# Rotating three key tiles on GpSimd and filling more TensorE waits with unread products in a fused attention and two-MLP kernel

## The chip, the core and the metric

One NeuronCore of a Trainium2 chip runs the whole program. The metric is the device time of one execution in microseconds (us), the median of several runs.

## What is computed

Attention with rotated queries and keys for 4 batches of 8 heads (576 tokens, 64 columns per head), then a two-layer MLP behind a layer norm (512 to 2048 to 512, with a residual), then a second, gated MLP that mixes tokens. All in fp32. The part that the change touches is the attention:

```python
def rotate(x):
    x1, x2 = (x[..., :half], x[..., half:])
    return np.concatenate([x1 * cos - x2 * sin, x1 * sin + x2 * cos], axis=-1)
q_rot, k_rot = (rotate(q), rotate(k))
scores = scale * np.matmul(q_rot, k_rot.transpose(0, 1, 3, 2))
scores = scores - np.max(scores, axis=-1, keepdims=True)
attn = np.exp(scores)
attn = attn / (np.sum(attn, axis=-1, keepdims=True) + 1e-09)
return np.matmul(attn, v)
```

## The kernel before

**Work.** A batch is a "group" g (0 to 3; batch 1 of the title is g = 0). Its 8 heads are 4 head pairs p; two heads lie on partitions 0 to 63 and 64 to 127. The queries of a pair are cut into hi = 0 (tokens 0 to 383, three units of 128) and hi = 1 (tokens 384 to 575, one unit of 128 and one of 64, which holds both heads as `qd`). A block is one pair and one half. In batch 1 the blocks run in the order hi = 0 for pairs 1 to 4 (blocks 0 to 3), then hi = 1 for pairs 1 to 4; in the other batches both halves of a pair follow each other. Only hi = 0 blocks load and rotate keys, so blocks 0 to 3 hold all the keys of batch 1.

**One unit.** TensorE (PE) makes the scores S of each head (L300, two products of 288 columns into the one PSUM tile of that head, S0 or S1). VectorE (DVE) takes the row maximum (L328). ScalarE (ACT) writes exp(S - max) into P with the row sums (L337), which frees the score tile. PE transposes P in blocks (L372) into the one PSUM tile T, ACT copies T to PT (L396, L403, L407), and when all of a block is there PE multiplies with the values (PV, L473). In the hi = 0 blocks of batch 1 (`ALONE`) the two heads of a unit run one after the other, the PV tile is one of the two PSUM tiles `m` of the MLP (`mps`), and the reciprocals of the row sums come by three PE transposes (inv, L491) and a multiplication on DVE (L496). In all other blocks they go to DRAM and back through DMAs on the GpSimd (POOL) queue (L436 to L447), and DVE multiplies at L484.

**Keys and queries.** `k_task` in `prep` loads both halves of a pair's keys as `kin` (L207, SP queue, two buffers), multiplies with cos and sin (L218, 1152 columns), adds the two halves into K (L220, 576 columns) and writes a second copy of the last 64 tokens (L226). The kin buffer is given back after that. `q_task` does the like for the queries (L252, L255, L263). All of it is on DVE.

**Around it.** 32 pieces of the MLP weights come in double precision and are turned into two fp32r parts (`convert`: ACT L58, L60, L733, DVE L62, L735, with loads `cd` and stores `wsc` on SP). When the four hi = 0 blocks of batch 1 are done, the layer norm of its first 288 tokens starts (`ln`: PE L604 with the ones matrix into the T tile, DVE L609, L618, ACT L629); the first MLP products follow (`up`, L754 to L756, then `down`, L784 to L786).

**What sets the order.** Everything is recorded by a planner (`Sched`) that runs while the kernel is built. Each task tells its engine, its earliest time and a cost in us; the planner always takes the step that can start first, and among those that could start within a fraction of it the one of lower rank. `UNIT`, `TURN`, `EVAC`, `VAL`, `NORM` and `REST` hold these ranks by batch: scores, transposes, copies of T, values, layer norm. The order so found is fixed on each engine; on the chip an instruction waits for its semaphores, and whatever is behind it on its engine waits too. Where the planner foresees that PE will wait, it calls `steady`, which records products of the `ones` matrix whose result nobody reads: 18 at the start, and later as many as the foreseen wait allows at 0.11 us each. They go into the `m` tiles. Before the change it does so only until the first values product has been recorded (`attn.pv`).

Of the kernel before, what the change touches and what calls it, by code (L numbers as in the profile page):

```python
# [10 lines left out]
ALU = mybir.AluOpType  # L11
# [11 lines left out]
FILL = 18  # L23
HOLD = 0.3
SWITCH = 0.3
ALONE = ((0, 0),)
UNIT = [2.25, 2.5, 2.25, 1.25]
EVEN = [9, 1, 1, -1]
RANK = dict(end=-1, convert=4.5, prep=3, load=3.5, loader=0.25)
NORM, REST = [0, 0.25, 1.5, 4], [2.75, 2.25, 3.5, 2.75]  # L30
TURN, EVAC, VAL = [2.25, 2.5, 2.5, 4.5], [1.25, 1.5, 0.25, 0.5], [2.75, 0.25, 1.75, 0.75]
FG = [4, 8, 8, 4]

AHEAD = 2
# [108 lines left out]
def latest(*xs):  # L143

    return None if any(x is None for x in xs) else max(xs)


class Attn:
# [42 lines left out]
    def prep(self, bi):  # L191

        nc, c, B = self.nc, self.c, self.blocks[bi]
        cs = self.k["cs"]
        parts = list(zip(KC, KC[1:])) if bi == 0 else [(0, 576)]
        s0, s1 = SPAN[B["hi"]]
        n = s1 - s0

        def k_task():
            e = yield "SP", self.kin.free, 0.7  # L200
            slot = self.kin.take()
            kin = self.p.tile([128, 2, 576], F32, tag="kin", name="kin")
            at = []
            for i, (a, z) in enumerate(parts):
                if i:
                    e = yield "SP", 0.0, 0.7
                nc.sync.dma_start(out=kin[:, :, a:z], in_=self.k["k"][B["b"], B["p"]][:, :, a:z])  # L207
                at.append(e + (3.5 if len(parts) > 1 else 7.5))
                if bi == 0:
                    e = yield "SP", 0.0, 0.6  # L210
                    q_load(*((0, 128), (128, 384))[i])
            for i, (a, z) in enumerate(parts):
                yield "DVE", lambda: latest(at[i], self.K.free() if i == 0 else 0.0), 0.0
                if i == 0:
                    B["kslot"] = self.K.take()
                    B["K"] = self.p.tile([128, 640], F32, tag="K", name="K", bufs=KB)
                yield "DVE", 0.0, 0.15 + 0.0021 * (z - a)
                nc.vector.tensor_tensor(kin[:, :, a:z], kin[:, :, a:z], cs[:, :, a:z], ALU.mult)  # L218
                e = yield "DVE", 0.0, 0.15 + 0.00105 * (z - a)
                nc.vector.tensor_tensor(B["K"][:, 64 + a:64 + z], kin[:, 0, a:z], kin[:, 1, a:z], ALU.add)  # L220
                if bi == 0:
                    if i == 0:
                        B["k0"] = e + 0.1
                        yield from q_turn((0, 128), at[0] + 0.6)
            e = yield "DVE", 0.0, 0.22
            nc.vector.tensor_tensor(B["K"][64:128, 0:64], kin[64:128, 0, 512:576], kin[64:128, 1, 512:576], ALU.add)  # L226
            B["k"] = e + 0.1
            self.kin.give(slot, e)
            if bi == 0:
                yield from q_turn((128, 384), at[1] + 0.6)  # L230

        def q_load(a=0, z=n):
            if a == 0:
                B["qslot"] = self.qin.take()
                B["Q"] = self.p.tile([128, 2, 384], F32, tag="qin", name="qin", bufs=QB)
            nc.sync.dma_start(out=B["Q"][:, :, a:z], in_=self.k["q"][B["b"], B["p"]][:, :, s0 + a:s0 + z])

        def q_turn(span, at):
            a, z = span
            t = B["Q"]  # L240
            yield "DVE", at, 0.15 + 0.0021 * (z - a)
            nc.vector.scalar_tensor_tensor(t[:, :, a:z], t[:, :, a:z], 0.125, cs[:, :, s0 + a:s0 + z], op0=ALU.mult, op1=ALU.mult)
            e = yield "DVE", 0.0, 0.15 + 0.00105 * (z - a)
            nc.vector.tensor_tensor(t[:, 0, a:z], t[:, 0, a:z], t[:, 1, a:z], ALU.add)
            B["q" if a else "q0"] = e + 0.1
# [20 lines left out]
        if B["newk"]:  # L266
            c.task(k_task(), 0.1 if bi == 0 else RANK["prep"] + 0.01 + 0.02 * bi)
# [16 lines left out]
    def unit(self, i, heads=None):  # L284
# [28 lines left out]
        if not after:  # L313
            c.task(self.unit(i, (1,)), UNIT[g])
        if after:
# [7 lines left out]
            if i + 1 < len(self.units):  # L323
                c.task(self.unit(i + 1), UNIT[self.units[i + 1]["g"]])
        nb, at = u["nb"], u["at"]
# [198 lines left out]
def fused_kernel(ctx, tc, q, k, v, cs, cst, w12, wi, wo, wsg, wsg4, gb, out):  # L524
    nc = tc.nc
    B = q.shape[0]
# [35 lines left out]
    mpsb = Bank(2)  # L562
    attn_ctx = ExitStack()
    attn = Attn(tc, attn_ctx, dict(q=q, k=k, v=v, cs=csb, ident=ident, x0=get_x0, x0_free=x0_free, mps=mps, mpsb=mpsb, dram=dram), groups, C)
# [8 lines left out]

    def steady(a, z):

        if attn.pv or z - a < 0.25:
            return
        n, r = (FILL, 128) if a < 1.0 else (int((z - a - 0.1) / 0.11), 64)
        for i in range(n):
            if i % 4 == 0:  # L580
                ps = mps.tile([128, 512], F32, tag="m", name="m")
            c = 128 * (i % 4)
            nc.tensor.matmul(ps[:, c:c + 128], ones[0:r], ones[0:r], start=True, stop=True)
# [104 lines left out]
    for g in range(NG):  # L688
        n = FG[g]
# [539 lines left out]
```

## Time and profile before

| | us |
|---|---|
| median of 3 runs (lowest, highest) | 916.14 (915.33, 917.90) |
| the profiled execution | 921.93 |
| its span, first to last instruction | 920.2 |

| engine | busy us (share of the span) | instructions |
|---|---|---|
| PE, matmul | 905.6 (98%) | 7206 |
| PE, weight load | 794.9 (86%) | 7206 |
| DVE | 586.0 (64%) | 1226 |
| ACT | 496.9 (54%) | 1132 |
| POOL | 107.4 (12%) | 212 |

The chain of waits that ended last is PE for 93% of the span. A busy PE is not the same as a PE at its peak: the ends of products are modelled, and short waits between them count as busy. A timeline row gives start, duration, engine, line, operation, tiles and shape, the count of records merged into it, and in brackets the idle time before it with what ended that. An fp32 product that is written once in the program shows as two records.

### The profile page before, as it was taken

The numbers are of one execution on the slowest core, as the hardware profiler recorded it, in microseconds if no ns is written. First come the engines' busy times: TensorE is split into PE (matmuls) and PEld (weight loads), VectorE is DVE, ScalarE is ACT, GpSimd is POOL, SyncE is SP. The second block draws the span as 40 slices with busy tenths as digits, with TensorE's granted clock in tenths as the row PEclk, the third lists the DMA queues.
The fourth block names the chain that finished last, engine by engine and source line by source line (L and its number), as shares of the span: only waits on it lengthen the run. The fifth ranks groups of instructions, "written<-read, shape, count | busy, mean of one in ns | idle before, by whom it ended". The sixth has DMA issues, their size and how long they took to land.

```text
span 920.2 us, 18252 instructions
## 1 busy us (share of the span) xinstructions
PE 905.6 (98%) x7206; PEld 794.9 (86%) x7206; DVE 586.0 (64%) x1226; ACT 496.9 (54%) x1132; POOL 107.4 (12%) x212
## 2 busy tenths in 40 slices
PE   9998999999999999999999999999999999999998
PEld 8556777777997887899778889999999999999998
DVE  6868776867686644358665316763435887776754
ACT  4989878768336655534455533464313746373520
POOL 0004321223001322300313220000000000000000
PEclk9989999999999999999999999999999999999999
DMA  8456536666472644257426333988651201203011
GB/s 319 164 181 226 197 111 218 214 231 240 186 223 74 199 146 139 80 187 236 136 77 213 101 105 122 325 287 273 211 178 40 65 2 50 66 1 104 1 52 53
DMA packets 64854, 138.81 MB, mean 151 GB/s; under 512 B 13056, under 2 KB 36224, under 8 KB 64768
## 3 DMA queue, kind: packets, MB, share of 16 engines
q1 hardware_dynamic: 57152, 132.96, 43.0%
q0 software_dynamic: 6784, 4.01, 1.8%
q8 instruction: 57, 0.93, 0.4%
q10 hardware_dynamic: 832, 0.66, 0.2%
q14 instruction: 29, 0.24, 0.1%
HBM read 110.43 MB, written 26.28 MB: 149 GB/s over the span
## 4 chain that ended last, share of the span: by engine, by line
PE 93%; ACT 4%; DMA 1%; DVE 1%; issue 0%; POOL 0%; POOLq 0%; DVEq 0%
PE S L300 10%; PE PV L473 8%; PE m L754 8%; PE m L784 8%; PE m L785 7%; PE m L786 7%; PE m L756 7%; PE m L755 7%; PE T L372 5%; PE p L1062 2%; PE p L1060 2%; PE p L1061 2%; PE p L1159 2%; PE p L1160 2%; PE p L1144 2%; PE p L1143 2%
## 5 line engine op out<-in xcount | busy, mean ns | idle before, releaser
L328 DVE TENSOR_REDUCE nb<-S 128x1 f32<-128x576 f32 x144 | 103.9, 751 | 79.8 <-PE S L300 79.0
L754 PE MATMUL m<-xh,w 128*128 128x288 f32 x480 | 147.9, 308 | 2.8 <-DVE h L764 2.8
L784 PE MATMUL m<-h,w 128*128 128x288 f32 x480 | 146.7, 306 | 0.0
L785 PE MATMUL m<-h,w 128*128 128x288 f32 x480 | 142.3, 297 | 0.0
L755 PE MATMUL m<-xl,w 128*128 128x288 f32 x480 | 141.8, 295 | 0.1
L756 PE MATMUL m<-xh,w 128*128 128x288 f32 x480 | 141.1, 294 | 0.0
L786 PE MATMUL m<-h,w 128*128 128x288 f32 x480 | 140.7, 293 | 0.0
L396 ACT COPY PT<-T 128x1024 f32<-128x1024 f32 (+5 forms) x120 | 75.2, 647 | 79.7 <-PE T L372 79.3
L764 DVE SCALAR_TENSOR_TENSOR h<-m,h 128x288 fp32r<-128x288 f32 x128 | 58.4, 456 | 86.4 <-ACT h L762 85.6
L337 ACT ACTIVATE P<-S,nb 128x576 f32<-128x576 f32 x144 | 106.7, 745 | 11.7 <-DVE nb L328 11.0
L762 ACT ACTIVATE h<-m 128x288 fp32r<-128x288 f32 x128 | 52.4, 410 | 92.5 <-PE m L756 91.3
L300 PE MATMUL S<-K,qin 64*128 64x288 f32 x512 | 96.3, 434 | 5.8 <-ACT P L337 5.6
L754 PEld LDWEIGHTS m<-xh,w 128*128 128x128 f32 x480 | 89.9, 187 | 9.4 <-DVE h L764 4.6
L436 POOL DMA_DIRECT2D inv<-st x112 | 57.3, 518 | 334.7 <-DVE st L432 334.4
L784 PEld LDWEIGHTS m<-h,w 128*128 128x128 f32 x480 | 90.4, 188 | 5.8 <-issue 2.1
L785 PEld LDWEIGHTS m<-h,w 128*128 128x128 f32 x480 | 90.8, 189 | 0.3
L755 PEld LDWEIGHTS m<-xl,w 128*128 128x128 f32 x480 | 90.2, 188 | 0.9 <-DVE xl L618 0.3
L786 PEld LDWEIGHTS m<-h,w 128*128 128x128 f32 x480 | 90.6, 189 | 0.0
L756 PEld LDWEIGHTS m<-xh,w 128*128 128x128 f32 x480 | 90.3, 188 | 0.0
L473 PE MATMUL PV<-PT,vin 128*64 128x384 f32 (+1 forms) x640 | 88.6, 419 | 0.0
L372 PEld LDWEIGHTS T<-ident,P 64*128 64x128 f32 x1312 | 58.7, 139 | 22.9 <-issue 8.8
L300 PEld LDWEIGHTS S<-K,qin 64*128 64x128 f32 x512 | 51.1, 188 | 25.2 <-ACT P L337 10.4
(154 smaller groups left out, 1849.6 us busy)
## 6 DMA issues: line engine op xcount, KB each, us to landing
w<-wsc SPq DMA_DIRECT2D x96, 512.0 KB, 4.0
cd<-in_w SPq DMA_DIRECT2D x32, 512.0 KB, 5.2
wsc<-w SPq DMA_DIRECT2D x24, 512.0 KB, 4.1
kin<-in_k SPq DMA_DIRECT2D x15, 576.0 KB, 6.4
vin<-in_v SPq DMA_DIRECT2D x20, 320.0 KB, 4.2
qin<-in_q SPq DMA_DIRECT2D x15, 384.0 KB, 6.3
x1d<-x SPq DMA_DIRECT2D x32, 144.0 KB, 2.8
x<-x1d SPq DMA_DIRECT2D x32, 144.0 KB, 2.8
```

The costliest lines, as they stand in the source:

```text
L300: nc.tensor.matmul(S[j][:, n, :], q, Kb["K"][r, a:a + HQ], start=True, stop=True)
L328: nc.vector.tensor_reduce(nb[:, j:j + 1], S[j], AX.XY, ALU.max, negate=True)
L337: nc.scalar.activation(P[:, 576 * j:576 * j + 576].rearrange("p (n k) -> p n k", n=2), S[j], AF.Exp, bias=nb[:, j:j + 1], scale=1.0, accum ...
L372: nc.tensor.transpose(ps[:, j, 64 * n:64 * n + 64], x["tile"][r, 128 * i:128 * i + 128], self.k["ident"][r, r])
L396: copy(t[:, i:i + n, q0:q0 + 128].rearrange("p c (j q) -> p j c q", j=2), ps[:, :, 64 * s:64 * s + 64 * n].rearrange("p j (c q) -> p j c q ...
L473: nc.tensor.matmul(ps[r, 0:n], V["vin"][:, ch, r], t[:, 4 if ch == 4 else 5 * j + ch, 0:n], start=ch == 0, stop=ch == 4)
L754: nc.tensor.matmul(ps, w[:, 0, ms], xh[:, kc, :], start=kc == 0, stop=False)
L755: nc.tensor.matmul(ps, w[:, 0, ms], xl[:, kc, :], start=False, stop=False)
L756: nc.tensor.matmul(ps, w[:, 1, ms], xh[:, kc, :], start=False, stop=kc == 3)
L784: nc.tensor.matmul(ps, w[:, 0, ms], t[:, 0, :], start=a == 0, stop=False)
L785: nc.tensor.matmul(ps, w[:, 1, ms], t[:, 0, :], start=False, stop=False)
L786: nc.tensor.matmul(ps, w[:, 0, ms], t[:, 1, :], start=False, stop=a == n - 1)
```

## The change

```diff
--- before.py
+++ after.py
@@ -24,11 +24,12 @@
 HOLD = 0.3
 SWITCH = 0.3
 ALONE = ((0, 0),)
-UNIT = [2.25, 2.5, 2.25, 1.25]
+GK = (1, 2, 3)
+UNIT = [2.25, 1.75, 2.25, 1.25]
 EVEN = [9, 1, 1, -1]
 RANK = dict(end=-1, convert=4.5, prep=3, load=3.5, loader=0.25)
 NORM, REST = [0, 0.25, 1.5, 4], [2.75, 2.25, 3.5, 2.75]
-TURN, EVAC, VAL = [2.25, 2.5, 2.5, 4.5], [1.25, 1.5, 0.25, 0.5], [2.75, 0.25, 1.75, 0.75]
+TURN, EVAC, VAL = [2.25, 2.5, 2.5, 4.5], [-1, 1.5, 0.25, 0.5], [2.75, 0.25, 1.75, 0.75]
 FG = [4, 8, 8, 4]
 
 AHEAD = 2
@@ -197,6 +198,7 @@
         n = s1 - s0
 
         def k_task():
+            eng, ve, f = ("POOL", nc.gpsimd, 2.0) if bi in GK else ("DVE", nc.vector, 1.0)
             e = yield "SP", self.kin.free, 0.7
             slot = self.kin.take()
             kin = self.p.tile([128, 2, 576], F32, tag="kin", name="kin")
@@ -210,20 +212,20 @@
                     e = yield "SP", 0.0, 0.6
                     q_load(*((0, 128), (128, 384))[i])
             for i, (a, z) in enumerate(parts):
-                yield "DVE", lambda: latest(at[i], self.K.free() if i == 0 else 0.0), 0.0
+                yield eng, lambda: latest(at[i], self.K.free() if i == 0 else 0.0), 0.0
                 if i == 0:
                     B["kslot"] = self.K.take()
                     B["K"] = self.p.tile([128, 640], F32, tag="K", name="K", bufs=KB)
-                yield "DVE", 0.0, 0.15 + 0.0021 * (z - a)
-                nc.vector.tensor_tensor(kin[:, :, a:z], kin[:, :, a:z], cs[:, :, a:z], ALU.mult)
-                e = yield "DVE", 0.0, 0.15 + 0.00105 * (z - a)
-                nc.vector.tensor_tensor(B["K"][:, 64 + a:64 + z], kin[:, 0, a:z], kin[:, 1, a:z], ALU.add)
+                yield eng, 0.0, f * (0.15 + 0.0021 * (z - a))
+                ve.tensor_tensor(kin[:, :, a:z], kin[:, :, a:z], cs[:, :, a:z], ALU.mult)
+                e = yield eng, 0.0, f * (0.15 + 0.00105 * (z - a))
+                ve.tensor_tensor(B["K"][:, 64 + a:64 + z], kin[:, 0, a:z], kin[:, 1, a:z], ALU.add)
                 if bi == 0:
                     if i == 0:
                         B["k0"] = e + 0.1
                         yield from q_turn((0, 128), at[0] + 0.6)
-            e = yield "DVE", 0.0, 0.22
-            nc.vector.tensor_tensor(B["K"][64:128, 0:64], kin[64:128, 0, 512:576], kin[64:128, 1, 512:576], ALU.add)
+            e = yield eng, 0.0, f * 0.22
+            ve.tensor_tensor(B["K"][64:128, 0:64], kin[64:128, 0, 512:576], kin[64:128, 1, 512:576], ALU.add)
             B["k"] = e + 0.1
             self.kin.give(slot, e)
             if bi == 0:
@@ -573,9 +575,9 @@
 
     def steady(a, z):
 
-        if attn.pv or z - a < 0.25:
+        if z - a < (0.5 if attn.pv else 0.25) or a > 130.0 or any(x is None or x > a for x in mpsb.at):
             return
-        n, r = (FILL, 128) if a < 1.0 else (int((z - a - 0.1) / 0.11), 64)
+        n, r = (FILL, 128) if a < 1.0 else (int((z - a - (0.2 if attn.pv else 0.1)) / 0.11), 64)
         for i in range(n):
             if i % 4 == 0:
                 ps = mps.tile([128, 512], F32, tag="m", name="m")
```

Three things change. The keys of blocks 1 to 3 (head pairs 2 to 4 of batch 1; `GK`) are rotated on GpSimd, with planned costs twice those of DVE. `steady` now also fills waits behind the first values product, if the foreseen wait is at least 0.5 us and both `m` tiles are free, up to a planned time of 130 us. Two ranks change: the copies of T in batch 1 come first of all (-1), and the scores of batch 2 come before its transposes (1.75). Lines in the changed file are two higher than in the one before (L300 is L302, L583 is L585).

The planner makes another order from it. On PE the unread products grow from 53 to 100; the other PE instructions are the same in number. Past the attention of batch 2 all five queues are in the same order as before.

PE, from the last transposes in front of the layer norm of batch 1 to its first MLP products. Before:

```order
L372 MATMUL T<-ident,P 128x64 x12
L300 MATMUL S_79<-K,qin 128x288
L300 MATMUL S_80<-K,qin 128x288
L604 MATMUL ln<-x_160,ones 128x288
L604 MATMUL ln<-x_288,ones 128x288
L604 MATMUL ln<-x_427,ones 128x288
L604 MATMUL ln<-x_595,ones 128x288
L300 MATMUL S_79<-K,qd_87 128x288 x2
L372 MATMUL T<-ident,P 128x64 x16
L754 MATMUL m<-xh,w 128x288
```

Now (L302 are the scores, L374 the transposes, L585 the unread products, L606 the layer norm, L756 the first `up` product):

```order
L302 MATMUL S_79<-K,qin 128x288
L302 MATMUL S_80<-K,qin 128x288
L585 MATMUL m<-ones 128x128 x16
L606 MATMUL ln<-x_160,ones 128x288
L606 MATMUL ln<-x_288,ones 128x288
L606 MATMUL ln<-x_426,ones 128x288
L606 MATMUL ln<-x_572,ones 128x288
L302 MATMUL S_79<-K,qd_87 128x288 x2
L585 MATMUL m<-ones 128x128 x9
L374 MATMUL T<-ident,P 128x64 x16
L585 MATMUL m<-ones 128x128 x7
L756 MATMUL m<-xh,w 128x288
```

Three runs of unread products, 16, 9 and 7, now stand where none stood: in front of the layer norm, behind the scores of `qd`, and in front of the first `up` products.

PE, the end of the hi = 0 blocks of batch 1. Before:

```order
L491 MATMUL inv<-ident,rb 128x128 x3
L372 MATMUL T<-ident,P 128x64 x8
L300 MATMUL S_79<-K,qin 128x288
L300 MATMUL S_80<-K,qin 128x288
L300 MATMUL S_79<-K,qin 128x288
L300 MATMUL S_80<-K,qin 128x288
L372 MATMUL T<-ident,P 128x64 x10
L473 MATMUL PV<-PT,vin_82 64x384 x6
L300 MATMUL S_79<-K,qd_86 128x288 x2
L372 MATMUL T<-ident,P 128x64 x16
```

Now:

```order
L302 MATMUL S_80<-K,qin 128x288 x2
L374 MATMUL T<-ident,P 128x64 x8
L585 MATMUL m<-ones 128x128 x15
L302 MATMUL S_79<-K,qin 128x288
L302 MATMUL S_80<-K,qin 128x288
L374 MATMUL T<-ident,P 128x64 x10
L302 MATMUL S_79<-K,qin 128x288
L302 MATMUL S_80<-K,qin 128x288
L585 MATMUL m<-ones 128x128 x5
L475 MATMUL PV<-PT,vin_82 64x384 x8
L302 MATMUL S_79<-K,qd_86 128x288 x2
L374 MATMUL T<-ident,P 128x64 x16
```

15 unread products stand between the transposes and the next scores, and 5 between scores and values; the three `inv` transposes of block 2 moved ahead of this piece, and eight instead of six values products follow in one run.

DVE, in the first units of batch 1, from the rotation of the queries of block 1 on. Before:

```order
L252 SCALAR_TENSOR_TENSOR qin<-qin,csb 128x768
L255 TENSOR_TENSOR qin<-qin 128x384
L328 TENSOR_REDUCE nb<-S_79 128x1
L218 TENSOR_TENSOR kin<-kin,csb 128x1152
L328 TENSOR_REDUCE nb<-S_80 128x1
L220 TENSOR_TENSOR K<-kin 128x576
L328 TENSOR_REDUCE nb<-S_79 128x1
L226 TENSOR_TENSOR K<-kin 64x64
L252 SCALAR_TENSOR_TENSOR qin<-qin,csb 128x768
L328 TENSOR_REDUCE nb<-S_80 128x1
L255 TENSOR_TENSOR qin<-qin 128x384
```

Now:

```order
L254 SCALAR_TENSOR_TENSOR qin<-qin,csb 128x768
L257 TENSOR_TENSOR qin<-qin 128x384
L330 TENSOR_REDUCE nb<-S_79 128x1
L330 TENSOR_REDUCE nb<-S_80 128x1
L254 SCALAR_TENSOR_TENSOR qin<-qin,csb 128x768
L257 TENSOR_TENSOR qin<-qin 128x384
L330 TENSOR_REDUCE nb<-S_79 128x1
L330 TENSOR_REDUCE nb<-S_80 128x1
L330 TENSOR_REDUCE nb<-S_79 128x1
```

The three key rows are gone from between the maxima; the query rotations stay. On POOL they stand directly behind the start of the program, ahead of all its DMAs:

```order
L892 MEMSET eps 128x1
L220 ISA
L220 TENSOR_TENSOR kin<-kin,csb 128x1152
L222 TENSOR_TENSOR K<-kin 128x576
L228 TENSOR_TENSOR K<-kin 64x64
```

The first row is a memset of the start; the ISA row, which stands there without a wait, is new too; the same three operations follow twice more (blocks 2 and 3), and then the DMA `inv<-st` (L438) that came right behind the memsets before.

## Rows read from the trace of the kernel before

**Rows 1.** One window: us, busy time (instructions) of each engine, PE clock, DMA share, GB/s.

```profile
43.64:57.40 13.76, 12.47 (x90) 6.64 (x87) 8.86 (x18) 10.49 (x23) 0.00 (x0) 0.75 0.49 176
```

**Rows 2.** Timeline of PE, the wait and the slow stretch at 45 to 53 us.

```profile
45.63 0.51 PE L300 MATMUL S<-K,qin 64*128 64x288 f32 x1 [1.29 <-ACT P L337]
...
46.52 1.90 PE L300 MATMUL S<-K,qin 64*128 64x288 f32 x5
...
53.30 0.58 PE L372 MATMUL T<-ident,P 64*128 64x64 f32 x10
```

**Rows 3.** Timeline of PE, from the last unit of hi = 0 to the first MLP products.

```profile
57.40 1.19 PE L300 MATMUL S<-K,qin 64*128 64x288 f32 x4
...
64.70 1.24 PE L300 MATMUL S<-K,qd 128*128 128x288 f32 x4
65.87 0.71 PE L372 MATMUL T<-ident,P 64*128 64x64 f32 x16
66.51 1.51 PE L473 MATMUL PV<-PT,vin 128*64 128x384 f32 x8
67.95 0.55 PE L491 MATMUL inv<-ident,rb 128*128 128x128 f32 x3
68.43 0.76 PE L300 MATMUL S<-K,qin 64*128 64x288 f32 x4
69.02 0.54 PE L372 MATMUL T<-ident,P 64*128 64x64 f32 x12
69.38 0.71 PE L300 MATMUL S<-K,qin 64*128 64x288 f32 x4
71.17 2.21 PE L604 MATMUL ln<-x,ones 128*128 128x288 f32 x8 [1.08 <-ACT PT L407]
...
75.02 0.71 PE L372 MATMUL T<-ident,P 64*128 64x64 f32 x16 [0.67 <-DVE xc L609]
...
77.95 0.76 PE L300 MATMUL S<-K,qin 64*128 64x288 f32 x4 [0.88 <-ACT P L337]
```

**Rows 4.** Timeline of PE in batch 2, its longest wait.

```profile
194.96 1.71 PE L300 MATMUL S<-K,qin 64*128 64x288 f32 x7 [1.93 <-ACT P L337]
```

**Rows 5.** Timeline of PE, a run of unread products.

```profile
10.21 2.28 PE L583 MATMUL m<-ones 64*128 64x128 f32 x19
12.33 0.65 PE L300 MATMUL S<-K,qin 64*128 64x288 f32 x2
```

**Rows 6.** Timeline of PE, the same pieces of a unit at full clock.

```profile
34.45 1.11 PE L300 MATMUL S<-K,qin 64*128 64x288 f32 x5
...
35.79 2.16 PE L473 MATMUL PV<-PT,vin 128*64 128x384 f32 x12
37.87 0.51 PE L300 MATMUL S<-K,qin 64*128 64x288 f32 x1
```

**Rows 7.** Timeline of DVE, the keys of block 1 between the maxima.

```profile
14.24 1.35 DVE L218 TENSOR_TENSOR kin<-kin,csb 128x1152 f32<-128x1152 f32 x1
15.51 0.75 DVE L328 TENSOR_REDUCE nb<-S 128x1 f32<-128x576 f32 x1
16.18 0.75 DVE L220 TENSOR_TENSOR K<-kin 128x576 f32<-128x576 f32 x1
...
17.95 0.22 DVE L226 TENSOR_TENSOR K<-kin 64x64 f32<-64x64 f32 x1
18.20 0.96 DVE L252 SCALAR_TENSOR_TENSOR qin<-qin,csb 128x768 f32<-128x768 f32 x1
```

**Rows 8.** Timeline of POOL, the largest memset.

```profile
0.74 0.20 POOL L884 MEMSET ones<- 128x128 f32 x1 [0.29 <-POOLq L1222]
```

**Rows 9.** Timeline of SP, the load of block 1's keys.

```profile
5.09 0.35 SPq L207 DMA_DIRECT2D kin<-in_k  x1
```

**Rows 10.** The key loads of line 207 in the first 30 us, issue to landing.

```profile
DMA to landing us min/median/max: 3.9/5.3/5.6
```

**Rows 11.** Window behind the wait of rows 4, columns as in rows 1.

```profile
196.00:200.00 4.00, 4.00 (x31) 3.65 (x28) 2.89 (x4) 4.00 (x8) 1.77 (x4) 0.60 0.72 206
```

## The prediction, made before the changed kernel ran

> **What bounds the kernel now.** I read the page first: PE is busy for 98% of the span and is 93% of the chain that ended last, so a change counts only by what it does to PE. Then windows by stage, to find where PE is not at its peak: from about 98 us on it is busy in nearly every window, but in the attention of batch 1 the row shows a granted clock of 0.75 in 13.76 us [rows 1]. The timeline of PE tells why: it waits 1.29 us for an exponential, and what follows runs slowly until 53.30 [rows 2]. Three more marked waits stand between 57 and 78 us, 1.08, 0.67 and 0.88 us [rows 3], and one of 1.93 us in batch 2 [rows 4]. Last I compared the orders: past the attention of batch 2 they agree, so what the change wins or loses on PE before about 240 us is the result, carried on by a busy PE.
>
> I divide batch 1 at two instants that both orders have: 12.33 (the first scores of the second unit), 57.40 (the scores of the second head of the last hi = 0 unit) and 77.95 (the scores behind the first six MLP products). Call 12.33 to 57.40 stretch A (45.07 us), 57.40 to 77.95 stretch B (20.55 us).
>
> **The price of an unread product.** 19 records take from 10.21 to 12.33 [rows 5], 0.112 us each. An fp32 product is two records, so one unread product takes 0.223 us, and a run that the code sized at 0.11 us per product lasts twice the wait that was foreseen. The order has 14 in stretch A where there were 19, and 52 in stretch B where there were none: 15, 5 and 16 up to the layer norm, 9 and 7 behind it.
>
> **Stretch B.** Work of PE from 57.40 to 71.17, by the distance of neighbouring starts [rows 3]: five score pairs at 0.59 (68.43 to 69.02) are 2.95; the `qd` scores 1.17; 16 transposes 0.64, 12 transposes 0.36, 18 more at the like rate about 0.65; 20 records of values at 0.18 (eight in 1.44) 3.6; six inverse transposes at 0.48 for three 0.96. The sum is 10.3 of 13.77 us, so 3.4 us are waits, marked or hidden in the modelled ends. Afterwards three inverse transposes have moved ahead, 9.85 us, and 36 unread products are 8.0 us: at least 17.9 us, 4.1 more. The products are longer than the waits they replace. In front of the layer norm PE waited 1.08 us for ACT's last copies of T; 16 products take 3.57 us. From 71.17 to 77.95 the time without the marked waits is 6.78 - 0.67 - 0.88 = 5.2 us; 16 products add 3.57, together 8.8, 2.0 more, or 1.5 if the first MLP products, which now start later, no longer wait for their low parts. I take +5.9 us for stretch B. This is a floor by PE's own work, whatever ACT and DVE do; it shrinks only if PE would have waited longer there than it does now.
>
> **Stretch A.** Four things.
> - The marked wait of 1.29 us [rows 2]. Its cycle has no values products between two pairs of scores. In the new order each cycle there has values, an inverse transpose or both; the poorest has only three inverse transposes (0.48 us). I count 1.29 off and 0.5 on.
> - The slow stretch. From 46.52 to 53.30 PE does in 6.78 us [rows 2] what it does from 34.45 to 37.87 in 3.42 us [rows 6]: five to six score records, eight transposes, twelve values records. That is 3.36 us. It came behind the wait and goes if no such wait comes back. I count it off.
> - Five unread products fewer, 1.1 us, if nothing else holds the first units.
> - Three inverse transposes that came in from stretch B, +0.48.
>
> Sum: -1.29 - 3.36 - 1.1 + 0.5 + 0.48 = -4.8 us.
>
> **What the keys on GpSimd do to that.** DVE loses 1.35 + 0.75 + 0.22 us [rows 7] three times, 7.0 us. The row maximum at 15.51 starts when the key product ends, and the next steps stand between maxima [rows 7]: this is the relief that lets the first units go with fewer unread products, and I give it no more than those 1.1 us, since behind 26 us PE's own work sets the pace. On POOL the trace has no two-input operation. Lower bound: DVE's own durations. Upper bound from the memset of 128 columns in 0.20 us [rows 8]: 1152 columns are 1.8 us in one pass, 3.6 with two inputs, and half of it, 1.8, for the sum. The keys of block 1 are issued at 5.09 [rows 9] and land 5.3 us later [rows 10], at 10.4; K is ready between 12.7 and about 16.3, against 18.17 on DVE. So not late even at the upper end, and I charge nothing; the two other pairs are needed 8 us apart each. The load of block 3's keys waits on SP for this buffer, was issued at 18.2 and comes no later now. On POOL the first normaliser DMA came at 69.33, long after. The ISA row is ahead of the first product and has the 9 us in which POOL waits for the keys. If that cover fails, K is late by as much and PE stands in the fourth unit.
>
> **A rule that speaks against the change.** No row shows DVE and POOL reading at once. The query rotation of 0.96 us [rows 7] and the sum behind it stand in DVE's queue in front of the maxima, just while POOL would rotate keys. The Trainium skill (SBUF — State Buffer, section "Who interferes with whom") says that a DVE instruction with two SBUF inputs and a GpSimd instruction that reads SBUF exclude each other for a whole instruction, and that reductions are free of it. No run here shows it. By it the relief would be given back; by the rows alone it stays. As a mechanism it is rival 2.
>
> **Sum.** -4.8 + 5.9 = +1.1 us. Batch 2's new rank only joins score pairs ahead of transposes, with the same products; I give it nothing. The profiled execution of 921.93 us would become 923.0; the median shown is 5.8 us below that execution, so I forecast 916.14 + 1.1 = 917.2 us. About 0.3% (2.7 us) is what a measurement of this kernel can tell from no change; this is inside.
>
> **Rivals.**
> 1. *The clock falls all the same* (slower). If the poorest cycle of stretch A makes PE wait as long as before (it decides from some 1.3 us on; the waits of 1.08 and 0.88 us [rows 3] were followed by no fall), the 3.36 us stay and 0.8 us of wait is back: +1.1 + 4.2 = +5.3, 921.4 us. For: both long waits of this kind, 1.29 and 1.93 us, were followed by a lower clock [rows 1, 11]. Against: the values are spread more evenly now.
> 2. *Query rotations behind POOL's key products* (slower). Two rotations of two operations each fall into POOL's work. Each may stand behind a product and a sum: between nothing and 2 x 5.4 us on DVE, against 4.5 us saved there in the same units. At half the wait, 5.4, the first units gain nothing and lose about 1 us: the 1.1 us are gone and +1 comes on top, 919.3 us; at the upper end 6.3 come on top instead, 924.6.
> 3. *The fills fit, and batch 2 runs through* (faster). The 1.93 us before 194.96 [rows 4] go, and with them the 0.60 clock behind [rows 11], which holds 4 us at 0.60 where 2.4 would do, 1.6 us. In batch 1 stretch A could give 1.7 us more if the freed DVE also shortens its cycles by 0.15 us in eleven units. Then +1.1 - 3.5 - 1.7 = -4.1, 912.0 us. Against: that wait hangs on a maximum behind a normaliser's DMA, and the order there has hardly changed.
> 4. *The change doesn't do what it says*: the keys come late from GpSimd, because its first product starts slowly, and PE stands in the fourth unit instead of being relieved. From 2 us of lateness on: +1.1 + 3, 920 us.
>
> **How the numbers follow.** Forecast 0.45 (from -1.5 to +2.7 us, the price of stretch B between 5.5 and 6.1 and stretch A between 3.4 and 6.5), rival 1 0.20, rival 2 0.12, rival 3 0.20, rival 4 0.03. Same 0.45, faster 0.20, slower 0.35. The range takes in rival 3 at its price and rival 1 with a little more, and leaves the upper ends of rival 2 and the sum of several out: 911.5 to 922.5.
>
> **What would show it.** In the new trace: the run of 16 unread products in 3.5 us with the layer norm directly behind it and no wait; some 18 us from the second-head scores to the layer norm instead of 13.77; the clock at 1.0 in all of batch 1; the instant 57.40 at about 52.6, that of the first scores behind the MLP products about 1 us later than 77.95; the wait before 194.96 still there. I am wrong if waits remain beside the unread products (then they cost less than 0.223 us each), if the clock in batch 1 falls again, if DVE's query rotations show long durations beside POOL's products, or if the two traces drift apart behind 100 us.

## The result, and the profile after

The changed kernel takes 931.01 us (median of 4 executions, 929.11 to 932.39) against 917.02 for the kernel before on the same chip (4 executions, 915.33 to 920.99): ratio 1.0146, 95% interval 1.0115 to 1.0177. It is 1.5% slower, with the whole interval above 1, and outside the forecast range. The profiled execution took 931.6 us, 9.7 more than the profiled one of before.

The page of the changed kernel, its span and its row for PE:

```profile
span 929.8 us, 18451 instructions
PE 915.4 (98%) x7300; PEld 809.9 (87%) x7300; DVE 584.8 (63%) x1217; ACT 496.9 (53%) x1132; POOL 121.6 (13%) x221
```

PE is still busy for 98% of a span that has grown by 9.6 us, so the loss is inside what counts as busy. The windows of the changed kernel tell where (columns as in [rows 1]):

```profile
12.23:17.90 5.67, 3.75 (x38) 2.94 (x36) 5.63 (x5) 1.83 (x6) 5.43 (x4) 1.00 1.04 417
17.90:20.00 2.10, 2.10 (x14) 1.60 (x14) 2.10 (x1) 1.27 (x3) 2.02 (x2) 0.63 1.03 422
20.00:35.50 15.50, 15.50 (x92) 11.76 (x91) 5.96 (x10) 7.87 (x17) 6.12 (x5) 0.50 0.14 44
...
37.00:63.11 26.11, 25.12 (x229) 15.14 (x226) 19.89 (x39) 24.63 (x55) 0.00 (x0) 1.00 0.55 187
63.11:90.31 27.20, 26.63 (x237) 21.46 (x233) 17.06 (x39) 20.68 (x47) 4.28 (x8) 1.00 0.68 229
200.00:220.00 20.00, 20.00 (x197) 17.68 (x196) 16.90 (x34) 16.18 (x38) 6.07 (x12) 1.00 0.75 266
```

The clock stands at its lower level, 0.50 (1.2 of 2.4 GHz), from about 20 to 35.5 us; the slow stretch of [rows 1] at 45 to 53 us is gone. So are the wait of [rows 4] and the slow stretch of [rows 11], whose place, 117 us behind the end of stretch B, now lies near 207 us: PE has no idle time between 200 and 220. With the prediction's instants, stretch A is 63.11 - 12.23 = 50.88 us (before 45.07), stretch B is 90.31 - 63.11 = 27.20 (before 20.55), and the rest of the span is 2.86 us shorter. 5.81 + 6.65 - 2.86 is the 9.6. The timeline of PE in the changed kernel, ahead of the slow stretch and in stretch B:

```profile
12.23 0.65 PE L302 MATMUL S<-K,qin 64*128 64x288 f32 x2
...
14.65 1.33 PE L585 MATMUL m<-ones 64*128 64x128 f32 x10
17.90 0.84 PE L302 MATMUL S<-K,qin 64*128 64x288 f32 x2 [1.93 <-ACT P L339]
...
63.11 1.19 PE L302 MATMUL S<-K,qin 64*128 64x288 f32 x4
...
64.36 3.45 PE L585 MATMUL m<-ones 64*128 64x128 f32 x29
...
78.25 3.73 PE L585 MATMUL m<-ones 64*128 64x128 f32 x32
81.91 2.21 PE L606 MATMUL ln<-x,ones 128*128 128x288 f32 x8
...
90.31 0.76 PE L302 MATMUL S<-K,qin 64*128 64x288 f32 x4
```

PE waits 1.93 us for an exponential of the second unit, and the 0.50 begins behind it. In stretch B 16 products (32 records) take 3.66 us up to the layer norm, which has no wait of its own any more, as foreseen. The exponential is late because of DVE; its timeline in the changed kernel:

```profile
11.59 3.05 DVE L254 SCALAR_TENSOR_TENSOR qin<-qin,csb 128x768 f32<-128x768 f32 x1
14.68 1.64 DVE L257 TENSOR_TENSOR qin<-qin 128x384 f32<-128x384 f32 x1
16.24 1.41 DVE L330 TENSOR_REDUCE nb<-S 128x1 f32<-128x576 f32 x2
17.57 2.43 DVE L254 SCALAR_TENSOR_TENSOR qin<-qin,csb 128x768 f32<-128x768 f32 x1
20.04 1.64 DVE L257 TENSOR_TENSOR qin<-qin 128x384 f32<-128x384 f32 x1
```

and that of POOL:

```profile
11.21 2.62 POOL L220 TENSOR_TENSOR kin<-kin,csb 128x1152 f32<-128x1152 f32 x1 [9.75 <-DMA vin<-in_v]
13.90 2.00 POOL L222 TENSOR_TENSOR K<-kin 128x576 f32<-128x576 f32 x1
15.98 0.52 POOL L228 TENSOR_TENSOR K<-kin 64x64 f32<-64x64 f32 x1
16.57 2.62 POOL L220 TENSOR_TENSOR kin<-kin,csb 128x1152 f32<-128x1152 f32 x1
19.27 2.00 POOL L222 TENSOR_TENSOR K<-kin 128x576 f32<-128x576 f32 x1
...
22.95 2.61 POOL L220 TENSOR_TENSOR kin<-kin,csb 128x1152 f32<-128x1152 f32 x1 [1.09 <-DMA kin<-in_k]
25.64 1.41 POOL L222 TENSOR_TENSOR K<-kin 128x576 f32<-128x576 f32 x1
```

The query rotation that took 0.96 us [rows 7] takes 3.05 and 2.43, its sum 1.64 for 0.56. Each of these four ends 0.4 to 0.8 us behind the end of the POOL operation beside it, as if it did most of its work only then. DVE starts a unit's maxima only when POOL's two long operations are through (16.24). The maxima themselves keep their 0.7 us each. POOL pays as well: its sum takes 2.00 beside DVE's rotations and 1.41 for the third pair, where DVE rotates nothing.

### The profile page after: what moved, and what is told of

It reads as the page before. It is cut to its first block, busy times and chain, and to the rows that moved or that the text cites. A ratio compares the mean times of both kernels' runs of the same rounds, so it can differ in the third digit from the quotient of the medians.

```text
span 929.8 us, 18451 instructions
## 1 busy us (share of the span) xinstructions
PE 915.4 (98%) x7300; PEld 809.9 (87%) x7300; DVE 584.8 (63%) x1217; ACT 496.9 (53%) x1132; POOL 121.6 (13%) x221
## 4 chain that ended last, share of the span: by engine, by line
PE 93%; ACT 2%; DMA 2%; DVE 1%; issue 1%; POOL 0%; SPq 0%; POOLq 0%; DVEq 0%
PE S L302 10%; PE PV L475 8%; PE m L786 8%; PE m L756 7%; PE m L787 7%; PE m L788 7%; PE m L757 7%; PE m L758 7%; PE T L374 5%; PE m L585 2%; PE p L1064 2%; PE p L1062 2%; PE p L1063 2%; PE p L1161 2%; PE p L1162 2%; PE p L1145 2%
## 5 line engine op out<-in xcount | busy, mean ns | idle before, releaser
L756 PE MATMUL m<-xh,w 128*128 128x288 f32 x480 | 148.2, 309 | 2.8 <-DVE h L766 2.8
L302 PE MATMUL S<-K,qin 64*128 64x288 f32 x512 | 98.0, 443 | 5.1 <-ACT P L339 4.7
L438 POOL DMA_DIRECT2D inv<-st x112 | 57.1, 517 | 326.9 <-DVE st L434 326.8
L756 PEld LDWEIGHTS m<-xh,w 128*128 128x128 f32 x480 | 90.1, 188 | 8.6 <-DVE h L766 4.2
L475 PE MATMUL PV<-PT,vin 128*64 128x384 f32 (+1 forms) x640 | 86.5, 414 | 1.0 <-ACT PT L398 1.0
L374 PEld LDWEIGHTS T<-ident,P 64*128 64x128 f32 x1312 | 60.6, 141 | 21.7 <-issue 8.4
L302 PEld LDWEIGHTS S<-K,qin 64*128 64x128 f32 x512 | 53.6, 193 | 24.9 <-issue 9.0
```

What stands on the lines that cost most here:

```text
L302: nc.tensor.matmul(S[j][:, n, :], q, Kb["K"][r, a:a + HQ], start=True, stop=True)
L374: nc.tensor.transpose(ps[:, j, 64 * n:64 * n + 64], x["tile"][r, 128 * i:128 * i + 128], self.k["ident"][r, r])
L475: nc.tensor.matmul(ps[r, 0:n], V["vin"][:, ch, r], t[:, 4 if ch == 4 else 5 * j + ch, 0:n], start=ch == 0, stop=ch == 4)
L756: nc.tensor.matmul(ps, w[:, 0, ms], xh[:, kc, :], start=kc == 0, stop=False)
```

## The experiments

No kernel here leaves out a part of the computation; unread products and the scratch work on GpSimd are only added or taken away. The runs have short names, e1 to g2. Ratios are to the kernel before, measured together with each run: 918.08 us (914.42 to 922.49, 13 executions) for e1 to e4, then 917.62, 916.32 and 916.90 (23 executions each) for the later groups. These medians of one kernel differ by up to 1.8 us, so a difference between runs of different groups, and any to the changed kernel's 931.01, is uncertain by about as much.

**The parts alone.** Theory: the keys on GpSimd cost by shutting DVE out, the late products by being twice as long as their waits. Rival: the new order of the units costs.

```
- eng, ve, f = ("POOL", nc.gpsimd, 2.0) if bi in GK else ...
+ eng, ve, f = ("POOL", nc.vector, 2.0) if bi in GK else ...
```

The planner still counts the keys on POOL, so the order on PE is that of the change (e1).

> The changed kernel with its order unchanged, but the nine key operations of blocks 1 to 3 are issued on DVE at the places that the planner gave them on GpSimd; all unread products stay. Theory (keys on GpSimd hold DVE's query rotations, PE waits 1.93 us at 16 us, and its clock is at the lower level until 35 us): the query rotation of 768 elements takes 0.95 us again instead of 3.05 and 2.43, the wait before the third unit shrinks below 0.6 us, the granted clock from 16 to 35 us is 1.0, and the scores behind the first six MLP products start at 82 to 85 us instead of 90.31; about 924 us. Rival (the unread products are the whole loss, the keys cost nothing): within 2 us of the changed kernel's 931. Second rival (DVE now has 7 us more to do in the first units and is late itself): 928 or more, with the rotations at 0.95 us but maxima late behind key operations.

Measured: 922.53 us (922.47 to 922.81), ratio 1.0059 (1.0042 to 1.0076), 8.5 below the changed kernel. DVE's timeline has the rotations back at their old durations, and the clock is at 1.00 in stretch A and B (windows of this kernel):

```profile
11.89 0.94 DVE L254 SCALAR_TENSOR_TENSOR qin<-qin,csb 128x768 f32<-128x768 f32 x1
12.87 0.56 DVE L257 TENSOR_TENSOR qin<-qin 128x384 f32<-128x384 f32 x1
```

```profile
12.52:54.51 41.99, 40.85 (x382) 26.97 (x380) 35.38 (x63) 36.76 (x81) 0.00 (x0) 1.00 0.57 207
54.51:81.70 27.19, 26.62 (x237) 21.44 (x233) 17.05 (x39) 20.70 (x47) 4.25 (x8) 1.00 0.68 230
```

Stretch A falls to 41.99 us, 3.1 below before; B stays at 27.19. So the keys' place does all of its harm in stretch A, as the theory said, and neither rival holds.

```
+ if attn.pv:
+     return
```

This line in `steady`, ahead of the count, leaves out every unread product behind the first values (e2).

> The changed kernel without the 52 unread products that stand behind the first values product; everything else in the same order, keys on GpSimd. Theory (both parts cost, the late products by 0.223 us each less the waits they cover): stretch A as in the changed kernel, 50.9 us, with the lower clock from 17.9 to 35 us; stretch B 20.5 to 22 us instead of 27.2; about 925 us. Rival (the late products are the whole loss of 14 us): 917 or 918 us. Second rival (the late products keep the clock up in stretch B, without them it falls there): a granted clock under 0.9 between 63 and 90 us and a gain of less than 4 us.

Measured: 927.03 us (926.77 to 928.72), ratio 1.0111 (1.0092 to 1.013), 4.0 below the changed kernel. Stretch B of its trace is 86.98 - 66.26 = 20.72 us, as the theory said. Stretch A is 66.26 - 12.56 = 53.70 instead of 50.9, with the clock at 0.50 from 18 to 40 us, so part of the gain was lost again there.

Both edits together (e4), which leaves the new order alone:

> Both together: keys on DVE at the planned places, and no unread products behind the first values product. What is left of the change is the order from the new ranks and costs. Theory: the two losses add up and nothing else is in the change, 917 to 919 us, level with the kernel before. Rival (the new order is itself worse in batch 2): 921 us or more, with new waits behind 95 us. Second rival (without any late product the clock falls in stretch A as it did before the change): a granted clock under 0.9 somewhere between 25 and 63 us, some 3 us above the sum of the two single gains.

Measured: 917.86 us (915.9 to 923.89, 11 executions), ratio 0.9996 (0.9975 to 1.0017). The new order alone is worth nothing that can be measured, and the two costs add: 8.5 to 9.2 us for the keys (changed kernel less e1, e2 less e4), 4.0 to 4.7 for the late products. The profiled execution, 923.89, was the longest of the eleven; in it the clock falls behind a wait at 57.33, as the second rival said (the rows stand in the last section).

**Is it GpSimd's reading?** In the kernel before, unread work on GpSimd beside the first rotations (lock_mul):

```
+ scr = self.p.tile([128, 512], F32, tag="scr", name="scr", bufs=1)
+ for i in range(12):
+     self.nc.gpsimd.tensor_tensor(scr, self.k["cs"][:, 0, 0:512], self.k["cs"][:, 1, 0:512], ALU.mult)
```

> The kernel before, with twelve unread two-input products of 512 columns on GpSimd from about 6 us on (rotation table times itself into a scratch tile), nothing else changed. Theory (DVE instructions with two SBUF inputs and GpSimd instructions that read SBUF shut each other out): DVE's key product (1.35 us before), key sum (0.75), query rotation (0.96) and its sum (0.56) in the first 25 us take 1.5 to 3 times as long, the row maxima (one input from PSUM) stay at 0.72, PE waits over 1 us in the first 25 us and the clock falls behind that wait. Rival (the loss in the changed kernel is not GpSimd's reading but the late keys or the order of PE): the DVE durations stay within 10% of before, no new wait.

Measured: 937.49 us, one execution. Its timelines of POOL and DVE:

```profile
6.18 19.63 POOL L519 TENSOR_TENSOR scr<-csb 128x512 f32<-128x512 f32 x12 [4.72 <-DMA csb<-in_cs]
```

```profile
12.61 1.78 DVE L242 SCALAR_TENSOR_TENSOR qin<-qin,csb 128x512 f32<-128x512 f32 x1
...
15.71 1.41 DVE L328 TENSOR_REDUCE nb<-S 128x1 f32<-128x576 f32 x2
17.05 2.02 DVE L252 SCALAR_TENSOR_TENSOR qin<-qin,csb 128x768 f32<-128x768 f32 x1
19.10 1.51 DVE L255 TENSOR_TENSOR qin<-qin 128x384 f32<-128x384 f32 x1
```

The twelve products follow each other every 1.64 us. The rotation of 768 elements that takes 0.96 us [rows 7] takes 2.02, that of 512 takes 1.78 (0.69 in the next kernel), each about 1.1 us more; the maxima are untouched. The sum at 19.10 takes 1.51 for 0.55 although it shares no tile with POOL's products, so it does not wait for their data. The effect is uneven: the key product of 1152 columns took 1.75 for 1.35, less than the theory said, and one of 576 columns kept its 0.75. PE then waits 1.79 us at 17.38 and the clock is 0.50 behind. The order of the kernel before suffers the same as the changed one, so no late key is needed for it. The same place with 18 `nc.gpsimd.memset(scr, 0.0)` (lock_memset):

> The kernel before, with eighteen unread memsets of 512 columns on GpSimd in the same place, which write SBUF and read nothing. Theory (what shuts DVE out is GpSimd's reading): DVE's key product, key sum, query rotation and its sum stay at 1.35, 0.75, 0.96 and 0.56 us within 10%, the span is that of before within 0.5%. Rival (any GpSimd access to SBUF does it): the same lengthening as with the products.

Measured: 916.13 us, one execution. POOL's memsets, and DVE beside them:

```profile
2.56 9.27 POOL L519 MEMSET scr<- 128x512 f32 x16
```

```profile
9.19 0.69 DVE L242 SCALAR_TENSOR_TENSOR qin<-qin,csb 128x512 f32<-128x512 f32 x1
```

Nothing is lengthened beside them: what holds DVE here is POOL's products, which read SBUF, and not its memsets, which only write it. (The memsets were over at 11.83, so they lay beside the first block's rotations only.)

**How much of it is the clock?** The changed kernel with nine more products in the run of five ahead of the 1.93 us wait (e3):

```
+ runs[0] += 1
+ n += 9 if runs[0] == 4 else 0
```

> The changed kernel with 9 more unread products in the run of 5 in front of the third unit's scores, where PE stood idle for 1.93 us; nothing else is different. Theory (the idle time makes the clock fall, and the lower clock until 35 us is a cost of its own): no idle time there, the granted clock stays at 1.0 from 16 to 35 us, stretch A shrinks from 50.9 us by 4 to 6 us; about 926 us. Rival (DVE's late maxima set the pace there, the clock follows from them and costs nothing itself): the clock is up, but PE waits for exponentials instead, and the time is within 1.5 us of 931.

Measured: 931.78 us (927.28 to 934.68), ratio 1.0155 (1.012 to 1.019). A miss: in the profiled execution the wait had moved to the next unit, and the clock fell behind it (timeline of PE, then a window of this kernel):

```profile
23.45 1.30 PE L302 MATMUL S<-K,qin 64*128 64x288 f32 x2 [1.85 <-ACT P L339]
```

```profile
24.00:36.00 12.00, 12.00 (x69) 8.45 (x68) 3.33 (x7) 6.51 (x14) 2.99 (x3) 0.50 0.01 1
```

DVE's second pair of lengthened rotations makes its own wait, which the first had hidden. One of the four executions kept a mean clock of 0.999 and took 927.28 us; the others, at 0.991 to 0.994, took 931.76 to 934.68. With `runs[0] in (4, 6)` both are filled (e5):

> The changed kernel (keys on GpSimd) with nine more unread products in each of the two runs of batch 1 that stand ahead of the waits of 1.93 us (in the changed kernel) and 1.85 us (in the kernel with the first of them filled): both waits are filled and the lengthened DVE instructions stay. Theory (most of the 8.5 us that the keys on GpSimd cost is the lower clock behind the wait, not the wait): no wait over 1 us in the first 40 us, the clock at 1.0 there, and 924.5 to 927.5 us, the 3.8 us of the filled waits above the 922.5 of the keys on DVE and 4 to 6 below the changed kernel. Rival (the wait moves on once more, and the clock falls behind it): a wait of 1.5 us or more behind 24 us, 0.5 for ten us or more, 930 to 933 us.

Measured: 925.71 us (925.29 to 928.18), ratio 1.0101 (1.0072 to 1.0129), stretch A in its windows:

```profile
12.47:58.21 45.74, 44.59 (x418) 31.03 (x416) 35.05 (x54) 36.72 (x81) 13.09 (x9) 1.00 0.52 190
```

Eighteen products more, the first rotation 2.56 us long and the other three lengthened instructions as long as in the changed kernel, and 5.3 us faster, as the theory said (4.1 by the ratios). Stretch A now separates: 41.99 with the keys on DVE, 3.75 for the waits that the shut-out DVE makes (45.74), 5.14 for the clock behind them (50.88). These are differences of single traces, good to about half a us.

**The late products at their true length.** Keys on DVE, and behind the first values `0.223` in place of `0.11` as the divisor: 24 products where there were 52 (f1).

> The changed kernel with the keys back on DVE at the same places of every order, and the unread products behind the values sized at the 0.223 us that one takes instead of 0.11: 24 where there were 52. Theory (the late products cost because they are twice as long as the waits they fill; half as many fill the wait and cost nothing): between 914.5 and 918.5 us, 4 to 6 below the 922.5 us with 52 products, the clock at 1.0 in all of batch 1. Rival (any product there delays the chain, because the foreseen waits are not there): about 920, half of the 4.7 us back. Second rival (half as many no longer hold the clock): waits of 0.7 us and more come back between 55 and 80 us, a stretch with a clock below 1.0, executions between 914 and 924.

Measured: 917.18 us (916.37 to 919.36, 12 executions), ratio 0.9997 (0.9979 to 1.0015), 5.35 below the 922.53 with 52. Stretch B is 21.35 us, 5.84 less than in e1: 28 products at 0.223 are 6.2, and 0.34 us came back as a marked wait. The clock is 1.00 throughout. This is the theory's outcome; the price per product is right, and the harm was the double count.

**One pair of keys on GpSimd.** As f1, with `nc.gpsimd if bi == 3 else nc.vector` (f2):

> As the kernel with the keys on DVE and 24 late products, but the keys of the fourth head pair (whose products on GpSimd lay beside no rotation of queries in the changed kernel) on GpSimd. Theory (only work of both engines on SBUF at the same time costs): GpSimd's product takes about 2.6 us, its sum 1.4, DVE's rotations stay under 1.0 us, and the time is that of the kernel with all keys on DVE within 1 us. Rival (a key rotation on GpSimd costs wherever it stands, some 2.8 us each, a third of the 8.5): about 2.8 us more.

Measured: 917.78 us (916.99 to 922.65, 10 executions), ratio 1.0013 (0.9991 to 1.0036), 0.6 above f1. POOL's product took 2.82 us and its sum 1.40. No query rotation lay beside it, but DVE's little 64 x 64 key sum did, and took 1.78 us for 0.22: between the theory and its rival, nearer to the theory.

**The early products too.** The divisor 0.223 for all of `steady`'s runs (f3):

> Keys on DVE, and all unread products that the code sizes by a wait, the early ones too, at 0.223 us each (before the values 13 where there were 30, behind them 24). Theory (a product more than the wait holds delays PE): 915 to 917 us, up to 2 below the 917.2 with only the late ones resized, the wait of 0.30 us before the scores at 22 us unchanged. Rival (the early runs lie beside DVE, which sets the pace there): the same 917.2 within 0.5 us, with marked waits in place of the products removed.

Measured: 922.79 us (9 executions, 916.95 to 926.81; a tenth, of 976.63 at a mean clock of 0.851, is left out), ratio 1.0062 (1.0032 to 1.0091). Both theories missed. The second unit starts 0.6 us earlier, as the theory said, but behind 1.10 us of waiting, and then (timeline of PE, and a window):

```profile
11.93 0.75 PE L302 MATMUL S<-K,qin 64*128 64x288 f32 x2 [1.10 <-ACT P L339]
```

```profile
14.00:35.00 21.00, 20.85 (x124) 14.73 (x124) 13.87 (x22) 11.68 (x26) 0.00 (x0) 0.51 0.40 146
```

The early runs are too long by the same factor, but their surplus of 0.6 us keeps PE from waiting, and the slow stretch that comes without it costs ten times that. The two shortest executions, 916.95 and 917.16, are no better than f1. Batch 2's rank put back (`UNIT[1]` = 2.5) in f1 (f4):

> Keys on DVE, 24 late products, and batch 2's rank of the score units put back to 2.5: batch 1 as the change orders it, batch 2 as before. Theory (the new rank of batch 2 costs some 1 to 1.4 us: from the scores behind the first MLP products to the end 839.4 us against 838.0 in the run of the kernel before with memsets, with a new wait of 0.96 us for ACT's PT): 915 to 916.5 us, all executions within 2 us. Rival (nothing in it, the difference is the state of the normaliser's DMA): 917.2 within 0.5 us. Second rival (the old rank brings back the wait of 1.93 us near 195 us of some executions): a spread of 5 us and more.

Measured: 917.97 us (917.0 to 918.67, 12 executions), ratio 1.0011 (0.9995 to 1.0026): the rank is worth nothing. With both edits (f5):

> The two last edits together. Theory: 914 to 916 us, below both kernels. Rival: no better than the best of the two alone.

Measured: 924.58 us (922.72 to 925.57), ratio 1.0081 (1.0058 to 1.0104), as f3 alone.

**What the slow stretch of before was worth.** The kernel before with six products in its wait of 1.29 us, nothing else: `steady`'s guard as in the change, and (g2)

```
+ if attn.pv:
+     late[0] += 1
+     n = 6 if late[0] == 1 else 0
```

> The kernel before, its order and its engines unchanged, with six unread products (1.34 us) in the wait of 1.29 us that PE has before the scores at 45.63. Theory (the lower clock follows the wait, so that filling it is worth the slow stretch): no wait over 1 us before the layer norm, the clock at 1.0 from 40 to 70 us, the scores behind the first MLP products at 74.3 to 75 instead of 76.3 (the run with memsets) to 77.95, and a median of 912.5 to 915 us where the kernel before shows about 917. Rival (the clock falls behind a later wait instead, as behind 0.96 us at 57.33 in the order without late products): the same 916 to 918, with a clock under 1.0 in a window between 55 and 80. Second rival (the spread of before comes from the normaliser's wait in batch 2): a median 1 to 2 us lower but a spread of 5 us or more.

Measured: 915.27 us (914.5 to 919.92, 13 executions), ratio 0.9972 (0.9953 to 0.9991): 1.6 us (0.28%) below the kernel before, an interval just clear of 1. The place of [rows 2] in its timeline and a window:

```profile
44.45 1.50 PE L588 MATMUL m<-ones 64*128 64x128 f32 x12
45.90 0.51 PE L300 MATMUL S<-K,qin 64*128 64x288 f32 x1
...
50.51 0.53 PE L372 MATMUL T<-ident,P 64*128 64x64 f32 x10
```

```profile
45.90:52.00 6.10, 6.10 (x60) 3.83 (x60) 4.57 (x12) 5.99 (x13) 0.00 (x0) 1.00 0.54 194
```

From the scores to the ten transposes it is 4.61 us where [rows 2] had 7.67: the lower clock follows the wait, and filling the wait removes it. The median stays 0.3 us short of the theory, perhaps because most executions of before lose less there than the profiled one (see "The base", below). The second rival fits too: the executions spread over 5.4 us, and the longest of them, the profiled one, has the wait of [rows 4] (timeline of PE):

```profile
192.66 2.31 PE L300 MATMUL S<-K,qin 64*128 64x288 f32 x7 [2.47 <-ACT P L337]
```

All five runs at 0.223 on the kernel before (g1):

> The kernel before with all five late runs sized at 0.223 us, 27 products: 7 in the wait of 1.29 us, 20 more between the last hi = 1 scores and the first MLP products, where before's marked waits are 1.08, 0.67 and 0.88 us. Theory (each product beyond a wait costs its 0.223 us): 20 x 0.223 = 4.5 us in the place of 2.6 us of waits, so 1.5 to 2 us above the kernel with one run, 914 to 917 us, executions within 2 us of each other but for the wait in batch 2. Rival (the layer norm's waits drop by as much, nothing lost): the same as with one run.

Measured: 915.86 us (915.01 to 917.21, 12 executions), ratio 0.9977 (0.9958 to 0.9996), 0.6 above g2 instead of the 1.5 to 2 expected. Stretch B is 21.33 us (75.53 - 54.20) against g2's 20.56 (75.12 - 54.56): 20 products, 4.5 us, took the place of 3.7 us of waiting, of which the marks show 2.3 (1.08 + 0.67 + 0.88, less 0.33 that stayed).

## Why the prediction was wrong

By its steps, for the profiled executions:

| step | forecast | measured |
|---|---|---|
| stretch B | +5.9 | +6.65 |
| stretch A | -4.8 | +5.81 |
| rest of the span | 0 | -2.86 |
| sum | +1.1 | +9.6 |

- **The price of a product** was right: 32 records took 3.66 us, 0.114 each, and stretch B came out 0.75 above its floor. Halving the products gave the surplus back (f1).
- **"So not late even at the upper end, and I charge nothing"** is the step that failed. The keys were in time: the product took 2.62 us, inside its bounds; the sum 1.41 alone but 2.00 beside DVE, above its bound of 1.8; block 1's K was whole at 16.50, 0.2 us past the upper end and ahead of the 18.17 on DVE. No wait named a late K. What was left out is that POOL's reading stretches the DVE instructions that stand beside it, by 2.11 + 1.08 + 1.49 + 1.09 = 5.8 us in two units (durations in the changed kernel less those in e1), more than the 4.6 us that left DVE there. The relief became a wait of 1.93 us. The prediction had named this sign itself, "if DVE's query rotations show long durations beside POOL's products". The prediction held the mechanism as rival 2, at 0.12, from the rule of the Trainium skill (SBUF — State Buffer, section "Who interferes with whom"). The trace now agrees with that rule in its three parts: two-input DVE work beside GpSimd's reading is held (1.1 to 2.1 us per instruction here), the maxima, reductions that read PSUM, are not (1.41 us for two), and memsets do no harm (0.69 us beside them). By the rows of before alone it could not be seen; a stated rule that speaks against a change needed more than 0.12 where the two kinds of work were known to lie side by side.
- **"It ... goes if no such wait comes back. I count it off"** was right for the old place: with the keys on DVE stretch A is 3.08 us shorter than before, and g2 shows 3.06 us from six products (the forecast said 3.36 for the stretch). It was wrong in the new place, where a longer wait brought some 16 us at 0.50. Of the 10.6 us by which stretch A missed, 3.75 are the waits, 5.14 the clock, and 1.7 that the gain was 3.08 and not 4.8. That term was too large: in e1's stretch A marked waits of 0.30 and 0.69 us stand in place of the 1.29, and what the five products fewer were worth was not separated.
- **The rivals were priced one at a time.** Rival 2 made the wait and rival 1, the fall of the clock, followed from it: 3.75 + 5.14 together. At half the wait rival 2 had 5.4 us on DVE, near the 5.8 measured, but put only 2.1 us on the time for it. Each alone was put 2 to 7 us above the forecast, and the range left "the sum of several out". A rival that makes PE wait can bring the fall of the clock with it, and its price has to hold both.
- **The base.** The profiled execution of before had the slow stretch of [rows 11] and the 1.93 us of [rows 4] in it, and was 4.9 us above the median of the call with the changed kernel. Not charging their loss while taking 5.8 off for the median counted that difference as if it were constant. In the execution with memsets, the same order on PE, the wait of 1.29 us was followed by less: the scores behind the first MLP products came at 76.34 instead of 77.95 [rows 3]:

```profile
76.34 0.76 PE L300 MATMUL S<-K,qin 64*128 64x288 f32 x4 [0.88 <-ACT P L337]
```

An execution like that one has 1.6 us less to give than the -1.29 and -3.36 that the prediction took off.
- **Batch 2's rank at nothing** was right (f4 against f1: 0.8 us more with the old rank, inside the noise).

What stays open: why the wait of [rows 4] appears in some executions and not in others; no run here was aimed at it. The lengthened rotations were not tried with the queries rotated on GpSimd too.

## What to carry to other kernels

Before moving an elementwise step to GpSimd to relieve DVE, list what DVE reads from SBUF in the same microseconds. Here its two-input instructions were held by up to about one GpSimd instruction each (0.56 became 1.64 us, 0.96 up to 3.05), so long GpSimd instructions hurt short DVE ones; reductions from PSUM kept their time, and memsets on GpSimd did no harm. A copy can be held too (last section). Price an unread product from a timeline row, by the records that one product makes, and remember that errors in it are not symmetric: a surplus costs its own length (28 products, 5.35 us), a shortage can cost a slow stretch (0.6 us saved, some 6 us lost in f3). Where a trace shows a wait followed by a lower granted clock, fill that one wait first and leave the order alone: here six products in one wait saved 1.6 us, while the whole change lost 14.

## What the runs showed that was not expected

**The length of a wait does not tell whether the clock falls.** In the kernel with the order alone PE waited 0.96 us and ran at 0.50 behind it (timeline and windows of e4):

```profile
57.33 0.84 PE L302 MATMUL S<-K,qin 64*128 64x288 f32 x1 [0.96 <-ACT P L339]
```

```profile
58.00:60.00 2.00, 2.00 (x13) 1.17 (x11) 0.78 (x3) 1.14 (x3) 0.00 (x0) 0.50 0.88 286
60.00:64.00 4.00, 4.00 (x13) 1.48 (x14) 2.63 (x4) 3.70 (x9) 0.00 (x0) 0.50 0.69 240
```

In e2 the same wait of 0.96 us in the same place was followed by full clock (the window of e2 lies around it):

```profile
69.17 0.51 PE L302 MATMUL S<-K,qin 64*128 64x288 f32 x1 [0.96 <-ACT P L339]
```

```profile
68.00:72.00 4.00, 3.04 (x24) 1.67 (x25) 3.55 (x9) 3.94 (x8) 0.00 (x0) 1.00 0.71 227
```

and in the kernel before a wait of 1.21 us between MLP products and scores was followed by full clock:

```profile
96.90 1.24 PE L300 MATMUL S<-K,qin 64*128 64x288 f32 x8 [1.21 <-ACT P L337]
```

```profile
97.00:99.00 2.00, 2.00 (x23) 1.43 (x24) 0.81 (x3) 1.84 (x5) 1.99 (x4) 1.00 0.42 148
```

So rival 1's "from some 1.3 us on" was no boundary. What does decide, no run here shows.

**The kernel before is short when it holds the clock.** Of its 82 executions beside these runs, the 23 with a mean clock of 1.000 took 914.16 to 917.73 us, the 9 at 0.994 took 921.03 to 922.77. Kernels that hold the clock often repeat themselves, the four executions of e1 within 0.34 us and the twelve of g1 within 2.2, but not always: e5 ran at 0.999 and 1.000 and spread over 2.9.

**A slow stretch outlives its wait.** Behind 1.10 us it lasted some 21 us in f3, behind 1.93 some 16 in the changed kernel, against 7 in the kernel before behind 1.29.

**DVE's copies can be held too.** In e5 a copy of the reciprocals, with one SBUF input, stood beside POOL's sum of the third pair (25.55 to 26.95) and took 1.38 us, where the changed kernel and e1 show 0.36 (timeline of DVE):

```profile
25.78 1.38 DVE L429 COPY rb<-su 128x384 f32<-128x384 f32 x1
```

So two SBUF inputs are not the only case to look for; this is one instruction of one run, and no run was aimed at it.
